# Scales of the input weights made for two blocks at once on GpSimd, with other paces beside the first attention

## The chip, the cores and the metric

One core of a Trainium2 chip runs the kernel. The core's engines each work through a queue of their own in order: TensorE (PE, matmuls; its weight loads are the row PEld), VectorE (DVE), ScalarE (ACT), GpSimd (POOL) and SyncE (SP, which here only issues DMAs; ACT issues some too). The metric is the device time of one execution in microseconds (us), the median of several runs.

## The reference, cut to what matters

Eight batches of sliding-window attention (8 heads, 576 positions, head size 64, window 128, a slope per head as bias), and on its output a bilinear feed-forward layer:

```python
scores = scale * np.matmul(q, k.transpose(0, 1, 3, 2))
mask = (rel >= 0) & (rel < window)
scores = np.where(mask, scores + bias[None], -1000000000.0)
attn = np.exp(scores - np.max(scores, axis=-1, keepdims=True))
attn = attn / (np.sum(attn, axis=-1, keepdims=True) + 1e-09)
...
x = attn_out.transpose(0, 2, 1, 3).reshape(B * S, H * D)   # attn_out = attn @ v
a = x @ w_a
b = x @ w_b
return (a * b @ w_out).astype(np.float32)
```

The float32 operands of most matmuls are split into two float16 parts, high and low, and a product is three matmuls (high by high, high by low, low by high). Each operand is first multiplied by a power of two that is made from its own norms.

## The kernel before

**Stages.** `first_attention` does batch 0's attention, four pairs of heads (p = 0 to 3) in four banks each, 16 turns in all. `first_batch` then runs the feed-forward layer of batch 0: `first_up` (12 blocks f of 128 hidden columns, 48 matmuls each, 576 in all, 49 steps), then `first_down` (24 steps of 12 matmuls). `batch(b)` does the same for batches 1 to 7. Beside the feed-forward layer of batch b runs the attention of later batches, `attention()`, in seventh parts of a pair of heads; `Pace.along(main, n, place)` steps it so that it stands at `place` pairs when the n steps of `main` are over. `weave(main, (side, a, z, steps))` spreads `steps` steps of `side` over the steps a to z of `main`.

**Weights.** The generator `weights` prepares the 12 blocks of the input weights (`up_weights`) and then the output weights (`down_weights`). It is stepped beside `first_attention` (`other(0.5)` is called 36 times and takes `rate` times a half step each time: 39 steps at a rate of 2.2), and then in `first_batch`. A block f goes through these stages:

- its two matrices are loaded (`load_weights`, L115, 512 KB each, from ACT's queue after the first three blocks) and put together from 64-bit words: ACT L126, DVE L127 and L129, two additions on POOL (L131);
- ACT squares them (L137), and PE adds the squares over the rows by four matmuls with ones (`up_norms`, L153, into a PSUM tile `wn_ps`);
- DVE takes the maximum of each matrix (L157, a reduction to `wtop`), and `power_scale` makes two scales of it in `sup`: L107 (clamp, factor), L109 (shift to the exponent), L110 (back to a float), all three on two columns;
- ACT writes the two high parts with the scale (L145), DVE the two low parts (L146, behind a pair of additions in `rest`).

**What sets the order.** Each engine's order is set when the kernel is compiled: a scheduler places instructions by its own simulated times. SP's order is written by hand in `first_attention` and `first_batch`, and PE's from batch 1 on; everything else is the scheduler's, so that a changed pace in one place can change the order of any engine nearby. `v`, the values of one batch for four pairs (1280 KB, L251), has one buffer: the next load waits until `split_x` has read what stands there. From batch 2 on, a pair's `qk` is split into `qkh` and `qkl` and laid out anew by four DMAs of SP's queue (L329 to L332), for which its score matmuls (L360) wait; `pT<-phl` (L383) is a transposing DMA of the probabilities.

## Time and profile before

| What | Value |
|---|---|
| median of 3 runs | 1061.12 us (1059.61 to 1067.57) |
| the profiled execution | 1065.21 us, its span 1063.4 us |
| PE busy | 991.9 us (93%) |
| DVE busy | 697.8 us (66%) |
| ACT busy | 649.3 us (61%) |
| POOL busy | 301.1 us (28%) |
| mean clock granted to PE | 0.973 of full speed |

The busy shares are means over the whole span. The stages differ: the views by window and by wait tell where PE, the busiest engine, stands still, and for whom. Times in the views are microseconds from the start of the span.

### The profile page before, as it was taken

The numbers are of one execution on the slowest core, as the hardware profiler recorded it, in microseconds if no ns is written. First come the engines' busy times: TensorE is split into PE (matmuls) and PEld (weight loads), VectorE is DVE, ScalarE is ACT, GpSimd is POOL, SyncE is SP. The second block draws the span as 40 slices with busy tenths as digits, with TensorE's granted clock in tenths as the row PEclk, the third lists the DMA queues.
The fourth block names the chain that finished last, engine by engine and source line by source line (L and its number), as shares of the span: only waits on it lengthen the run. The fifth ranks groups of instructions, "written<-read, shape, count | busy, mean of one in ns | idle before, by whom it ended". The sixth has DMA issues, their size and how long they took to land.

```text
span 1063.4 us, 23921 instructions
## 1 busy us (share of the span) xinstructions
PE 991.9 (93%) x9323; PEld 757.9 (71%) x9323; DVE 697.8 (66%) x1922; ACT 649.3 (61%) x1672; POOL 301.1 (28%) x331
## 2 busy tenths in 40 slices
PE   7678999979999899798999989999999989999998
PEld 5346667757776677575777767777777767777776
DVE  5999976446778646985777657775767576533530
ACT  6786777556767745666656666667656665523321
POOL 3444432100458304871112202230212212220110
PEclk8888999989999899998999999999999999999999
DMA  8344533653623633326423644335514733210000
GB/s 322 125 154 151 190 95 72 127 137 76 125 57 91 163 63 63 84 68 157 86 47 86 170 90 85 61 97 153 114 35 87 177 67 60 40 35 12 2 12 34
DMA packets 148433, 102.83 MB, mean 97 GB/s; under 512 B 120032, under 2 KB 128352, under 8 KB 147296
## 3 DMA queue, kind: packets, MB, share of 16 engines
q1 hardware_dynamic: 134496, 76.04, 31.6%
q10 hardware_dynamic: 13824, 25.27, 6.8%
q8 instruction: 73, 1.20, 0.5%
q14 instruction: 40, 0.33, 0.1%
HBM read 48.33 MB, written 9.44 MB: 54 GB/s over the span
## 4 chain that ended last, share of the span: by engine, by line
PE 46%; DVE 7%; ACT 7%; DMA 6%; issue 2%; SPq 0%; ACTq 0%; DVEq 0%
PE ch L776 15%; PE dn_ps L871 13%; PE p L776 11%; PE up_ps L776 3%; PE x_ps L473 2%; ACT phl L377 2%; DMA qk<-in_kT 2%; DMA v<-in_vP 2%; PE sc_ps L360 2%; DMA pT<-phl 1%; DVE phl L378 1%; DVE qkl L321 1%; ACT t L365 1%; ACT qkh L320 1%; DVE t L364 1%
## 5 line engine op out<-in xcount | busy, mean ns | idle before, releaser
L776 PEld LDWEIGHTS <-wup 128*128 128x128 f16 x4212 | 409.0, 99 | 145.5 <-issue 31.8
L871 PE MATMUL dn_ps<-h,wdn 128*128 128x288 f16 x2016 | 262.5, 289 | 2.3 <-DVE h L770 2.0
L776 PE MATMUL ch<-xs,wup 128*128 128x288 f16 x1584 | 231.1, 288 | 15.1 <-ACT rc L801 6.4
L871 PEld LDWEIGHTS <-wdn 128*128 128x128 f16 x2016 | 194.3, 99 | 58.1 <-issue 2.7
L776 PE MATMUL up_ps<-xs,wup 128*128 128x288 f16 x1440 | 189.1, 292 | 10.9 <-DVE v L590 4.1
L776 PE MATMUL p<-xs,wup 128*128 128x288 f16 x1188 | 178.9, 287 | 1.4 <-ACT rc L818 1.4
L365 ACT ACTIVATE t<-t,mn 128x192 f32<-128x192 f32 (+2 forms) x252 | 107.4, 427 | 73.6 <-DVE mn L364 72.8
L830 POOL TENSOR_TENSOR rc<-rc,row 128x288 f32<-128x288 f32 x66 | 60.1, 910 | 265.5 <-DVE row L828 233.7
L378 DVE SCALAR_TENSOR_TENSOR phl<-t,rin,phl 128x192 f16<-128x192 f32 (+2 forms) x252 | 105.9, 457 | 19.8 <-ACT phl L377 19.2
L377 ACT ACTIVATE phl<-t,rin 128x192 f16<-128x192 f32 (+2 forms) x252 | 88.9, 425 | 22.2 <-DMA pT<-phl 10.8
L769 ACT CAST h<-rc 128x576 f16<-128x576 f32 x96 | 64.0, 667 | 56.0 <-DVE rc L835 29.4
L770 DVE TENSOR_TENSOR h<-rc,h 128x576 f16<-128x576 f32 x90 | 73.0, 811 | 23.9 <-ACT h L769 22.7
L364 DVE CUSTOM_DVE_ANT_0 t<-sc_ps,bias,neg 128x192 f32<-128x192 f32 (+2 forms) x216 | 75.3, 389 | 19.6 <-PE sc_ps L360 19.5
L131 POOL TENSOR_TENSOR wup<-wup,wdn 128x512 int32<-128x512 int32 x36 | 51.9, 1464 | 66.1 <-ACT wdn L126 22.4
L408 DVE TENSOR_TENSOR xs<-v,xs 128x576 f16<-128x576 f32 x51 | 52.3, 1035 | 23.1 <-ACT xs L407 22.8
L807 DVE TENSOR_TENSOR rc<-p,rc 128x288 f32<-128x288 f32 x66 | 30.0, 455 | 52.6 <-PE p L776 50.8
L402 POOL TENSOR_TENSOR xq<-xq,sq 128x576 bf16<-128x576 bf16 x24 | 34.6, 1444 | 87.5 <-ACT sq L401 87.3
L875 ACT ACTIVATE row<-dn_ps,oi 128x288 f32<-128x288 f32 x56 | 27.6, 492 | 51.2 <-PE dn_ps L871 50.5
L812 ACT ACTIVATE row<-ch,g 128x288 f32<-128x288 f32 x66 | 32.6, 494 | 41.7 <-PE ch L776 41.2
L835 DVE SCALAR_TENSOR_TENSOR rc<-rc,g,ch 128x288 f32<-128x288 f32 x66 | 33.6, 509 | 35.1 <-PE ch L776 34.9
L360 PEld LDWEIGHTS <-qst 128*64 128x64 f16 x864 | 30.3, 110 | 32.4 <-issue 31.2
L234 POOL TENSOR_TENSOR wa<-wup 128x512 f32<-128x512 f16 x24 | 33.1, 1381 | 69.2 <-DVE phl L378 62.4
(137 smaller groups left out, 1337.2 us busy)
## 6 DMA issues: line engine op xcount, KB each, us to landing
v<-in_vP SPq DMA_DIRECT2D x8, 1280.0 KB, 6.6
out<-row ACTq DMA_DIRECT2D x64, 144.0 KB, 1.8
qk<-in_qT SPq DMA_DIRECT2D x28, 288.0 KB, 3.9
qk<-in_kT SPq DMA_DIRECT2D x28, 288.0 KB, 4.5
wdn<-in_w_out ACTq DMA_DIRECT2D x12, 512.0 KB, 5.3
wdn<-in_w_a ACTq DMA_DIRECT2D x9, 512.0 KB, 3.9
wdn<-in_w_b ACTq DMA_DIRECT2D x9, 512.0 KB, 4.8
qst<-qkh SPq DMA_DIRECT2D x24, 144.0 KB, 2.6
```

Of the source, the lines that this page charges most:

```text
L131: pool.tensor_tensor(out=t[:, m, :], in0=t[:, m, :], in1=low[:, m, :], op=ALU.add)
L360: pe.matmul(ps[64 * e:64 * e + 64, c:c + w], o.qs[:, e, qq], ks[:, e, kk], start=not last, stop=last)
L364: vec.tensor_tensor_reduce(out=t[:, c:c + w], in0=ps[:, c:c + w], in1=o.bias[:, WIN - w:WIN], scale=-0.125 if o.b == 1 else o.neg, scalar= ...
L365: act.activation(t[:, c:c + w], t[:, c:c + w], AF.Exp, bias=o.mn[:, n:n + 1], scale=-1.0, accum_out=o.sm[:, n:n + 1])
L377: act.activation(phl[:, 0, pc:pc + w], e, AF.Copy, scale=s)
L378: vec.scalar_tensor_tensor(out=phl[:, 1, pc:pc + w], in0=e, scalar=s, in1=phl[:, 0, pc:pc + w], op0=ALU.mult, op1=ALU.subtract)
L408: vec.tensor_tensor(out=xs[:, n, 1, :, :], in0=src, in1=xs[:, n, 0, :, :], op=ALU.subtract)
L769: act.copy(h[:, f, :, 0, :], hid)
L770: eng.tensor_tensor(out=h[:, f, :, 1, :], in0=hid, in1=h[:, f, :, 0, :], op=ALU.subtract)
L776: pe.matmul(ps[:, 0:HT], wup[:, a[0], a[1], wi, k, :], xs[:, b, xi, k, :], start=(first and n == 0), stop=(last and n == len(ks) - 1), ski ...
L830: pool.tensor_tensor(out=x0, in0=x0, in1=mid, op=ALU.mult)
L871: pe.matmul(ps[:, 0:HT], wdn[:, f, wi, e * P:(e + 1) * P], h[:, f, t, hi, :], start=(m == 0 and n == 0), stop=(m == NF - 1 and n == 2))
```

## The change

Scales are made for a group of two blocks: two blocks share one tile of PSUM, one reduction gives four columns, and `power_scale` runs on GpSimd (POOL), where the shift by 24 bits is a multiplication by 2^-24. The splitting of the two blocks, four pairs of instructions, follows over the next steps. `up_weights` has 56 steps in place of 52. The rate beside `first_attention` is 1.5 in place of 2.2 (27 steps in place of 39), the 50 steps beside `first_up` are spread over its steps 0 to 40 in place of 0 to 48, and the attention of batch 1 and 2 stands at 3.2 pairs in place of 2.8 after `first_up`, and at 5.15 in place of 4.9 after `first_down`. Line numbers behind the change are 4 or 5 higher: L126 is L130, L137 is L141, L145 is L149, L146 is L150, L157 is L161, L590 is L595.

```diff
--- before.py
+++ after.py
@@ -100,14 +100,18 @@
         vec.tensor_copy(c16, col)
         pe.matmul(dst, ones16, c16, start=True, stop=True)
 
-    def power_scale(dst, sq, slack, top):
+    def power_scale(dst, sq, slack, top, eng=vec):
 
         n = sq.shape[-1]
         cl = small.tile([P, n], F32, tag=f"cl{n}", name="cl")
-        vec.tensor_scalar(out=cl, in0=sq, scalar1=float(2.0**-40), scalar2=slack, op0=ALU.max, op1=ALU.mult)
+        eng.tensor_scalar(out=cl, in0=sq, scalar1=float(2.0**-40), scalar2=slack, op0=ALU.max, op1=ALU.mult)
         r = small.tile([P, n], I32, tag=f"r{n}", name="r")
-        vec.tensor_scalar(out=r, in0=cl.bitcast(I32), scalar1=24, scalar2=None, op0=ALU.logical_shift_right)
-        vec.tensor_scalar(out=dst.bitcast(I32), in0=r, scalar1=float(-(2**23)), scalar2=float((189 + top) * 2**23), op0=ALU.mult, op1=ALU.add)
+        if eng is pool:
+
+            eng.tensor_scalar(out=r, in0=cl.bitcast(I32), scalar1=float(2.0**-24), scalar2=None, op0=ALU.mult)
+        else:
+            eng.tensor_scalar(out=r, in0=cl.bitcast(I32), scalar1=24, scalar2=None, op0=ALU.logical_shift_right)
+        eng.tensor_scalar(out=dst.bitcast(I32), in0=r, scalar1=float(-(2**23)), scalar2=float((189 + top) * 2**23), op0=ALU.mult, op1=ALU.add)
 
 
     def load_weights(n, srcs, queue=act):
@@ -145,56 +149,57 @@
         act.activation(hi, x, AF.Copy, scale=s)
         return lambda: vec.scalar_tensor_tensor(out=lo, in0=x, scalar=s, in1=hi, op0=ALU.mult, op1=ALU.subtract)
 
-    def up_norms(f, sq):
-
-        ps = ps_at.tile([P, 512], F32, tag="at", name="wn_ps")
-        norms = ps[:, 0:2 * P].rearrange("p (m f) -> p m f", f=P)
+    def up_norms(f, sq, ps):
+
+        norms = ps[:, 2 * P * (f % 2):2 * P * (f % 2) + 2 * P].rearrange("p (m f) -> p m f", f=P)
         for c in range(NKC):
             pe.matmul(norms, ones16, sq[:, :, c * P:(c + 1) * P], start=(c == 0), stop=(c == NKC - 1))
 
-        def scale():
-            top = small.tile([P, 2], F32, tag="wtop", name="wtop")
-            vec.tensor_reduce(out=top, in_=norms, op=ALU.max, axis=AX)
-
-            power_scale(sup[:, f, :], top, 1.01, 14)
-
-        return scale
+    def up_scales(g, ps):
+
+        top = small.tile([P, 4], F32, tag="wtop", name="wtop")
+        vec.tensor_reduce(out=top, in_=ps.rearrange("p (m f) -> p m f", f=P), op=ALU.max, axis=AX)
+
+        power_scale(sup[:, 2 * g:2 * g + 2, :].rearrange("p f m -> p (f m)"), top, 1.01, 14, pool)
 
     def up_weights():
 
 
-        scale, sq, rest = {}, {}, []
-
-        def norms(f):
-            if f < NF:
-                scale[f] = up_norms(f, sq.pop(f))
-                if f + 3 < NF:
-                    load_weights(f + 3, (w_a[f + 3], w_b[f + 3]))
-                else:
-                    k = 2 * (f + 3 - NF)
-                    load_weights(f + 3, (w_out[k], w_out[k + 1]))
-
-        for f in range(NF + 1):
+
+        sq, rest, hi, ps = {}, [], [], None
+        for f in range(NF + 2):
             conv = convert(f) if f < NF else iter(())
             next(conv, None)
-            if f:
-                norms(f - 1)
+            n = f - 1
+            if 0 <= n < NF:
+                if n % 2 == 0:
+                    ps = ps_at.tile([P, 512], F32, tag="at", name="wn_ps")
+                up_norms(n, sq.pop(n), ps)
+                if n + 3 < NF:
+                    load_weights(n + 3, (w_a[n + 3], w_b[n + 3]))
+                else:
+                    k = 2 * (n + 3 - NF)
+                    load_weights(n + 3, (w_out[k], w_out[k + 1]))
             yield
             next(conv, None)
-            if f > 1:
+            if rest:
                 rest.pop(0)()
-            yield
-            if f:
-                scale.pop(f - 1)()
-                rest.append(split_up(f - 1, 0))
+            if 0 <= n < NF and n % 2:
+                up_scales(n // 2, ps)
+                hi += [(k, m) for k in (n - 1, n) for m in range(2)]
+            yield
+            if hi:
+                rest.append(split_up(*hi.pop(0)))
             yield
             if f < NF:
                 sq[f] = squares(f)
-            if f:
-                rest.append(split_up(f - 1, 1))
+            if hi:
+                rest.append(split_up(*hi.pop(0)))
+            if rest:
                 rest.pop(0)()
             yield
-        rest.pop(0)()
+        for _ in range(len(rest)):
+            rest.pop(0)()
 
     def down_weights():
 
@@ -917,7 +922,7 @@
     SP = {mybir.EngineType.SP}
     weights = chain(up_weights(), down_weights())
     with tc.manual_schedule(engines=SP):
-        first_attention(weights, 2.2)
+        first_attention(weights, 1.5)
     stack.close()
     hid = ctx.enter_context(tc.tile_pool(name="hid", bufs=1))
     h = hid.tile([P, NF, 2, 2, HT], F16, name="h")
@@ -936,8 +941,8 @@
         hidden_scale(st)
         for _ in split_x(st, True, False):
             pass
-        weave(att.along(first_up(st, h), 49, 2.8), (weights, 0, 48, 50))
-        weave(att.along(first_down(0, out_scale(st), h), 24, 4.9), (weights, 0, 12, 12))
+        weave(att.along(first_up(st, h), 49, 3.2), (weights, 0, 40, 50))
+        weave(att.along(first_down(0, out_scale(st), h), 24, 5.15), (weights, 0, 12, 12))
         for _ in weights:
             pass
 
```

**SP, the DMAs around the load of batch 2's values.** Before:

```order
L383 DMA_TRANSPOSE pT<-phl 128x32x128
L251 DMA v<-in_vP 128x2560
L329 DMA qst<-qkh 64x1152
L330 DMA qst<-qkl 64x1152
L331 DMA qkh<-qkh 64x1152
L332 DMA qkl<-qkl 64x1152
L293 DMA qk<-in_qT 64x2x576
L294 DMA qk<-in_kT 64x2x576
L383 DMA_TRANSPOSE pT<-phl 128x32x128
L293 DMA qk<-in_qT 64x2x576
L294 DMA qk<-in_kT 64x2x576
```

And now:

```order
L388 DMA_TRANSPOSE pT<-phl 128x32x128
L334 DMA qst<-qkh 64x1152
L335 DMA qst<-qkl 64x1152
L336 DMA qkh<-qkh 64x1152
L337 DMA qkl<-qkl 64x1152
L298 DMA qk<-in_qT 64x2x576
L299 DMA qk<-in_kT 64x2x576
L388 DMA_TRANSPOSE pT<-phl 128x32x128
L256 DMA v<-in_vP 128x2560
L298 DMA qk<-in_qT 64x2x576
L299 DMA qk<-in_kT 64x2x576
```

The load of `v` stands behind the four DMAs that lay out a pair, the two loads of `qk` and the transposing DMA; before, it stood ahead of all of them.

**ACT, the first pair of the first attention** (`vsq` is a sum of squares of `v`, of which four make its scale; `wdn<-in_w` are issued loads). Before:

```order
L260 ACTIVATE vsq,vs<-v 128x640
L137 ACTIVATE wdn<-wup 128x2x512
L260 ACTIVATE vsq,vs<-v 128x640
L585 COPY rin_397<-rin_ps 128x512
L585 COPY rin_397<-rin_ps 128x64
L115 DMA wdn<-in_w_a 128x512
L260 ACTIVATE vsq,vs<-v 128x640
L115 DMA wdn<-in_w_b 128x512
L126 ACTIVATE wdn<-wdn 128x1024
L145 ACTIVATE wup<-wup,sup 128x2x256 x2
L260 ACTIVATE vsq,vs<-v 128x640
L126 ACTIVATE wdn<-wdn 128x1024
```

And now:

```order
L265 ACTIVATE vsq,vs<-v 128x640
L141 ACTIVATE wdn<-wup 128x2x512
L265 ACTIVATE vsq,vs<-v 128x640
L590 COPY rin_363<-rin_ps 128x512
L590 COPY rin_363<-rin_ps 128x64
L265 ACTIVATE vsq,vs<-v 128x640
L130 ACTIVATE wdn<-wdn 128x1024
L265 ACTIVATE vsq,vs<-v 128x640
L130 ACTIVATE wdn<-wdn 128x1024
L141 ACTIVATE wdn<-wup 128x2x512
L119 DMA wdn<-in_w_a 128x512
L119 DMA wdn<-in_w_b 128x512
```

The two L145 and the two loads that stood ahead of the last `vsq` stand behind it, or later still.

**POOL and DVE, the last pair of the first attention** (L131, now L135, are the additions of a block; `cl`, `r` and `sup` the steps of a scale; L590, now L595, writes the attention's result into `v`). POOL before:

```order
L131 TENSOR_TENSOR wup<-wup,wdn 128x512 x2
L402 TENSOR_TENSOR xq<-xq,sq 128x576
L926 MEMSET phl 128x2x64
L926 MEMSET phl 128x2x128 x3
L926 MEMSET phl 128x2x64
L131 TENSOR_TENSOR wup<-wup,wdn 128x512 x2
```

POOL now:

```order
L407 TENSOR_TENSOR xq<-xq,sq 128x576
L135 TENSOR_TENSOR wup<-wup,wdn 128x512 x2
L107 TENSOR_SCALAR cl<-wtop 128x4
L931 MEMSET phl 128x2x64
L931 MEMSET phl 128x2x128 x3
L931 MEMSET phl 128x2x64
L111 TENSOR_SCALAR r<-cl 128x4
L135 TENSOR_TENSOR wup<-wup,wdn 128x512 x2
L114 TENSOR_SCALAR sup<-r 128x4
L407 TENSOR_TENSOR xq<-xq,sq 128x576 x2
```

DVE before, the end of the first attention:

```order
L129 SCALAR_TENSOR_TENSOR wup<-wdn,wup 128x2x512
L146 SCALAR_TENSOR_TENSOR wup<-wup,sup 128x2x256
L127 TENSOR_SCALAR wup<-wdn 128x2x512
L129 SCALAR_TENSOR_TENSOR wup<-wdn,wup 128x2x512
L157 TENSOR_REDUCE wtop<-wn_ps 128x2
L146 SCALAR_TENSOR_TENSOR wup<-wup,sup 128x2x256
L107 TENSOR_SCALAR cl<-wtop 128x2
L590 SCALAR_TENSOR_TENSOR v<-x_ps,sv,rin_845 128x512
L109 TENSOR_SCALAR r<-cl 128x2
L590 SCALAR_TENSOR_TENSOR v<-x_ps,sv,rin_845 128x64
```

DVE now:

```order
L131 TENSOR_SCALAR wup<-wdn 128x2x512
L580 RECIPROCAL rin_723<-rin_723 128x9
L133 SCALAR_TENSOR_TENSOR wup<-wdn,wup 128x2x512
L595 SCALAR_TENSOR_TENSOR v<-x_ps,sv,rin_659 128x512
L595 SCALAR_TENSOR_TENSOR v<-x_ps,sv,rin_659 128x64
L571 COPY pT<-tr_ps 128x512
L150 SCALAR_TENSOR_TENSOR wup<-wup,sup 128x2x256
L595 SCALAR_TENSOR_TENSOR v<-x_ps,sv,rin_746 128x512
L595 SCALAR_TENSOR_TENSOR v<-x_ps,sv,rin_746 128x64
```

The last step of the third group's scale (`sup<-r`) stands behind two additions of another block on POOL. On DVE, ahead of the last two L595, there stands one L150, which reads that scale.

## The prediction

> **What bounds the kernel now.** I began with the busy tenths of the page: over its 40 slices PE is full but for the first tenth of the span, and there DVE is the full one.
>
> ```profile
> PE   7678999979999899798999989999999989999998
> DVE  5999976446778646985777657775767576533530
> ```
>
> So I took the windows by stage: the end of the first pair of the first attention (25.5 us), the end of the first attention (89), and `first_up` to 181.3, in two parts and as a whole. The columns are busy us of PE, PEld, DVE, ACT and POOL, PE's granted clock and the DMA share.
>
> ```profile
> core 0: us, PE busy (x) PEld busy (x) DVE busy (x) ACT busy (x) POOL busy (x), PEclk, DMA share, GB/s
> 7.00:25.50 18.50, 12.08 (x124) 8.57 (x122) 13.37 (x38) 14.93 (x38) 5.95 (x5) 0.86 0.95 378
> 25.50:89.00 63.50, 42.40 (x387) 28.16 (x384) 60.35 (x138) 43.92 (x104) 31.66 (x27) 0.85 0.37 134
> 89.00:143.00 54.00, 50.03 (x409) 37.40 (x409) 46.20 (x115) 42.30 (x101) 20.04 (x14) 0.97 0.57 184
> 143.00:181.30 38.30, 38.30 (x361) 28.06 (x361) 27.65 (x80) 29.82 (x71) 10.17 (x9) 0.96 0.29 59
> 89.00:181.30 92.30, 88.33 (x769) 65.46 (x769) 73.85 (x193) 72.11 (x171) 30.21 (x23) 0.96 0.45 132
> ```
>
> From 25.5 to 89 us DVE works 60.35 of 63.50 us (95%), PE 42.40 and ACT 43.92: DVE is the bound there and PE is idle for 21 us. From 89 us PE is the bound: it idles 4.0 us up to 181.3. The two longest single waits of PE are in the view of waits (total, times, longest):
>
> ```profile
> PE vtot L267 <- DVE vc L264: 12.5, 4, 4.7
> ...
> PE sc_ps L360 <- DMA qkh<-qkh: 7.8, 2, 6.6
> ```
>
> The 4.7 us are the wait up to the first `vtot`, at 23.8 us, the 6.6 us for `qkh` lie at the start of batch 1, at 227.8 us. Behind that place the order of PE soon becomes the old one, so what is won or lost lies ahead of about 320 us, and the rest of the kernel moves with it.
>
> **Part 1: the first pair, -4.5 us.** PE's first scores of the second pair stand behind `vtot`, which waits for four sums of squares on ACT. ACT reached the last of them late:
>
> ```profile
> 18.10 0.74 ACT L260 ACTIVATE vsq<-v 128x640 bf16<-128x640 f32 x1 [1.62 <-DMA qk<-in_qT]
> ...
> 18.83 1.17 ACT L126 ACTIVATE wdn<-wdn 128x1024 int32<-128x1024 uint32 x1
> 19.86 1.35 ACT L145 ACTIVATE wup<-wup,sup 128x512 f16<-128x512 f32 x2
> 21.08 0.75 ACT L260 ACTIVATE vsq<-v 128x640 bf16<-128x640 f32 x1
> ...
> 23.54 0.16 DVE L264 CAST vc<-vs 128x4 bf16<-128x4 f32 x1
> ```
>
> In the new order the loads and the two L145 (1.62 us of waiting ahead of the third `vsq`, and 1.35) are behind the sums. ACT was free at 16.48 (18.10 less its wait): 0.74 + 1.17 + 0.75 more gives 19.1, in place of 23.54 when DVE, busy with L146, took them up. I take 4.5 us. At worst the second block's load is late and it is 3.
>
> **Part 2: the other three pairs, -11 us.** The DVE rows of the first 89 us that shrink:
>
> ```profile
> L129 DVE SCALAR_TENSOR_TENSOR wup<-wdn,wup 128x1024 int32<-128x1024 int32 x11 | 16.2, 1473 | 0.1
> L146 DVE SCALAR_TENSOR_TENSOR wup<-wup,sup 128x512 f16<-128x512 f32 x16 | 15.3, 958 | 3.0 <-ACT wup L145 3.0
> ...
> L127 DVE TENSOR_SCALAR wup<-wdn 128x1024 int32<-128x1024 int32 x11 | 8.4, 765 | 0.3 <-DMA wdn<-in_w_b 0.2
> L107 DVE TENSOR_SCALAR cl<-wtop 128x2 f32<-128x2 f32 x9 | 5.7, 630 | 0.1
> L109 DVE TENSOR_SCALAR r<-cl 128x2 int32<-128x2 int32 x9 | 4.1, 452 | 0.1
> L157 DVE TENSOR_REDUCE wtop<-wn_ps 128x2 f32<-128x256 f32 x9 | 3.7, 415 | 2.7 <-PE wn_ps L153 2.7
> L110 DVE TENSOR_SCALAR sup<-r 128x2 int32<-128x2 int32 x8 | 3.4, 429 | 0.1
> ```
>
> By the new order, three fewer each of L127 and L129 (0.765 + 1.473, 6.7 us) and seven fewer L146 (6.7) come before the end of this attention. All 26 instructions of the scales go to POOL (5.7 + 4.1 + 3.4 = 13.2). Nine reductions of 256 columns (3.7) become three of 512. A reduction of 512 columns and one of 64 take 0.81 together, so three cost at most 2.1, and that saves 1.6. In all DVE loses 28 us; about 4 of them lie ahead of 25.5 us, in part 1. DVE keeps 60.35 - 24 = 36 us. ACT loses two L126, two L137 and eight L145:
>
> ```profile
> L126 ACT ACTIVATE wdn<-wdn 128x1024 int32<-128x1024 uint32 x11 | 12.7, 1151 | 0.9 <-DMA wdn<-in_w_b 0.9
> ...
> L145 ACT ACTIVATE wup<-wup,sup 128x512 f16<-128x512 f32 x16 | 10.7, 718 | 1.7 <-DVE sup L110 1.7
> L137 ACT ACTIVATE wdn<-wup 128x1024 bf16<-128x1024 f32 x9 | 9.4, 1049 | 0.5 <-POOL wup L131 0.5
> ```
>
> This is 2.3 + 2.1 + 5.7 = 10, less the 1.35 of part 1: 35 us are left. PE keeps 42.40 less three blocks of norms (12 of the row below, 2.1 us): 40 us. So no engine is the bound by much; three share a chain (score, DVE, ACT, transpose, copy). If one engine could be 95% busy, as DVE was, the stretch would take 42 us. In the first stretch, where no engine led, the fullest was busy 14.93 of 18.5 (81%): 50 us. I add 2.5 us for a wait that the new order makes at the end. On DVE the last L595 stand behind an L150 that needs the third group's scale, and on POOL that scale stands behind two additions (2.5 us a pair in the last row below), then comes a scaling on ACT (0.7). I take 52.5 in place of 63.5. The ends are 42 (-21) and 61 (-2.5), three engines at 66%.
>
> ```profile
> L153 PE MATMUL wn_ps<-wdn,ones 128*128 128x256 bf16 x48 | 8.6, 311 | 3.0 <-ACT wdn L137 2.5 <-DVE mn L551 0.5
> 0.87 0.10 POOL L72 MEMSET halves<- 128x2 f32 x1
> ...
> 13.51 0.43 POOL L531 TENSOR_SCALAR bias<-rel_sb,sl_sb 128x192 f32<-128x192 f32 x1
> ...
> 28.71 2.52 POOL L131 TENSOR_TENSOR wup<-wup,wdn 128x512 int32<-128x512 int32 x2 [5.64 <-ACT t L552]
> ```
>
> The new work on POOL is 18 instructions of four columns. Between a memset of two columns (0.10) and a `tensor_scalar` of 192 (0.43) they cost 2 to 8 us in all, on an engine that is busy half of this stretch (31.66 of 63.50). I set it at nothing beside the 2.5 us above; its price is the waits in the third rival.
>
> **Part 3: `first_up`, +6 us.** What is deferred comes here: three blocks of norms on PE (+2.1, on the bound). DVE gets 13.4 us of L127, L129 and L146 more and 0.4 pairs of attention above 2.8 (about 3, if a third of the 73.85 was attention), less 2 for the scales: 73.85 + 15 = 89 of 94 us. ACT gets 10 and about 3: 85. Before, in 89 to 143, DVE was busy 46.2 of 54 (86%) and PE idle for 4.0, and from 143 to 181, at 72%, PE never waited. At 94% I expect about twice the idle time, 8 in place of 4. The ends are +2 (the norms alone) and +11 (DVE at 86%: 103.5 us for 92.3). The weights themselves come in time: in the new order the last norms stand behind 216 of the 576 matmuls of `first_up`, the output weights' total behind 474, which leaves 102 matmuls (13 us at 0.13, by the last row of part 4) ahead of `first_down`.
>
> **Part 4: the start of batch 1, -8 us.** SP's and PE's rows:
>
> ```profile
> 224.38 0.35 SPq L251 DMA_DIRECT2D v<-in_vP  x1
> ...
> 231.94 0.46 SPq L331 DMA_DIRECT2D qkh<-qkh  x1
> 234.54 6.53 SPq L383 DMA_TRANSPOSE pT<-phl  x1
> ...
> 252.30 0.51 SPq L329 DMA_DIRECT2D qst<-qkh  x1
> ...
> 255.51 0.51 SPq L332 DMA_DIRECT2D qkl<-qkl  x1
> ```
>
> ```profile
> 221.34 0.25 PE L360 MATMUL sc_ps<-qkl,qst 128*64 128x192 f16 x2
> ...
> 234.37 0.27 PE L360 MATMUL sc_ps<-qkh,qst 128*64 128x64 f16 x2 [6.55 <-DMA qkh<-qkh]
> ...
> 235.74 4.64 PE L776 MATMUL up_ps<-xs,wup 128*128 128x288 f16 x24
> ...
> 240.77 3.11 PE L776 MATMUL up_ps<-xs,wup 128*128 128x288 f16 x24
> ```
>
> At 224.38 the load of `v` got its buffer; the four layout DMAs were queued behind it (the third went out at 231.94 only), and PE stood for 6.55 us. In the new order they stand ahead of it. They then wait only for `qst`, which the matmuls of 221.34 release, and need some 6 us (252.30 to 255.51 for the four, and 2.4 to land, as from 231.94 to 234.37): 227.5. PE comes there 72 matmuls (0.13 each) after 221.6, at 231, and doesn't wait. With the wait goes the slower clock behind it (24 matmuls in 4.64, not 3.11). 6.55 + 1.5 is 8. The cost: `v` now goes out behind the transposing DMA (234.54 + 6.53, some 17 us later than before). In PE's order its first use, a `vtot`, stands 144 matmuls (19 us) and some scores behind those first scores, at 250 or later. `v` needs up to 7.6 us to arrive (224.38 to 231.94) and four sums of 0.75: 241 + 10.6 is about 252. This is close, but the transposing DMA was itself held up behind `v` and the layout before and can go out earlier. I take nothing. If `v` is late, the gain is gone. SP's queue behind `v` holds the next pair's loads, wanted a pair later.
>
> **The sum.** -4.5 - 11 + 6 - 8 = -17.5 us, so the profiled execution's 1065.2 would become 1047.7. That one lies 4.1 us over the median of the runs shown, so against the median 1061.1 I forecast 1043.6, rounded to 1044. The moved attention (0.25 pairs from batch 1 into batch 0's time) is the same PE work elsewhere: nothing, since both are bound by PE.
>
> **Rivals.**
> 1. Paid back in `first_up`: DVE or ACT becomes the bound there. For: 94% and 90% load in one stretch. Against: PE has five banks of slack there and stood only 4 us before. With parts 1 and 2 at -12, part 3 at +11 and part 4 at -8 it is -9: 1052.
> 2. The wait at the start of batch 1 only changes its name: `v` is late. For: SP's queue is in order, and `v` is behind a DMA that took 6.53 us of it. With part 4 at nothing it is -9.5: 1052.
> 3. Slower: the scales on POOL stand in ACT's way. ACT's four L149 of a group stand in its queue ahead of exponentials and of copies that free PE's banks, and all wait for POOL. The rows for the price:
>
> ```profile
> 28.95 1.07 DVE L107 TENSOR_SCALAR cl<-wtop 128x2 f32<-128x2 f32 x1
> ...
> 35.35 1.22 DVE L129 SCALAR_TENSOR_TENSOR wup<-wdn,wup 128x1024 int32<-128x1024 int32 x1
> ```
>
> A DVE instruction of two columns took 1.07 while POOL's two additions ran (from 28.71), and the cast of part 1, with four columns, 0.16: the two engines exclude each other. If each of a scale's three instructions waits out an L129 (1.22) and the group two additions (2.5), that is 6.2 us a group and 37 for six. This would give -17.5 + 37: 1081. It decides from 2.9 us shown on PE for each group. Against: only the third group has additions between its steps, and the splits stand one or more turns behind their reduction.
>
> The Trainium skill states this exclusion too (SBUF — State Buffer, section "Who interferes with whom"): the pair of ports that VectorE and GpSimd share is an exclusive lock, and a DVE instruction with two SBUF inputs contends with a GpSimd instruction that reads SBUF. The rows above agree. By that rule the lock that cost DVE 0.9 us at L107 now costs POOL, at the worst 18 times 1.22 or 22 us of its queue, and the time would be rival 3's only if all of that showed.
>
> **Chances and range.** The forecast (-11 us or more) 0.60; rival 1 0.17; rival 2 0.10; rival 3 0.08; losses or gains by the new order that I don't see 0.05, spread evenly. The likeliest time is 1044. With all ends of the parts at their best it is -4.5 - 21 + 2 - 8 = -31.5, with all at their worst -3 - 2.5 + 11 + 0 = +5.5. The low end of the range takes part 2 at -17 and part 3 at +3 (1034.6), the high end rivals 1 and 2 (1052) with part 2 worse by another 5: 1034 to 1057. About 1% (10.6 us) is what a measurement of this kernel can tell from no change: faster 0.62, same 0.28, slower 0.10.
>
> **What would show it.** Part 1: `vtot` near 19.3 us. Part 2: L595 of the last pair near 73 us, DVE no longer at 95%. Part 3: `first_up` lasts some 98 us, with DVE over 90%. Part 4: no wait of PE for `qkh` at the start of batch 1. The forecast is wrong if PE waits more than 15 us in `first_up`, or if ACT's L149 wait for `sup` in several groups.

## The result, and the profile after

| | before | after |
|---|---|---|
| time, median (range) of the runs | 1062.61 us (1059.61 to 1067.57, 7 runs) | 1054.47 us (1048.78 to 1058.66, 7 runs) |
| profiled execution, span | 1065.21, 1063.4 | 1050.78, 1049.0 |
| first `vtot` on PE | 23.75 | 19.46 |
| first attention's end (`up_ps` behind the last `v`) | 88.96 | 67.74 |
| first `dn_ps` (`first_down` begins) | 181.30 | 175.36 |
| first `up_ps` of batch 1 | 226.18 | 219.33 |
| first `dn_ps` of batch 1 (L871, now L876) | 317.30 | 305.22 |

The ratio is 0.9906 (95% interval 0.9877 to 0.9935). The kernel became 0.9% faster: 1054.5 lies in the range of the prediction, near its upper end, and 10 us over the forecast of 1044. By stages the two profiled executions differ by -4.3 (up to `vtot`), -16.9 (the rest of the first attention), +15.3 (`first_up`), -0.9 (`first_down`), -5.2 (batch 1 up to its `dn_ps`) and -2.3 behind that, in all -14.4. That is more than the -8.1 of the medians, since the profiled execution of before lies 2.6 over its median and that of after 3.7 under. Of all the runs below, one (1978.19 us, with the attention's place at 2.65) is in no median and no ratio.

The windows of after, cut at its own landmarks (columns as in the prediction):

```profile
core 0: us, PE busy (x) PEld busy (x) DVE busy (x) ACT busy (x) POOL busy (x), PEclk, DMA share, GB/s
20.20:67.74 47.54, 36.44 (x383) 24.99 (x380) 40.95 (x101) 40.95 (x101) 26.20 (x31) 0.89 0.39 142
67.74:175.36 107.62, 92.46 (x802) 67.63 (x801) 90.59 (x206) 80.16 (x188) 49.24 (x38) 0.95 0.56 143
```

From just behind `vtot` (20.20) to the end of the first attention DVE is busy 40.95 of 47.54 us (86%, it was 95%), and ACT exactly as long: the two are level now. `first_up` takes 107.62 us, and PE is idle for 15.2 of them (4.0 before), though DVE is busy only 84% and ACT 74%. Of the 15.3 us that this stage lost, 11.2 are idle time of PE. PE's largest waits, in the view of waits (total, times, longest):

```profile
PE up_ps L781 <- ACT rc L734: 7.9, 1, 7.9
...
PE rin_ps L586 <- DVE v L595: 4.3, 1, 4.3
...
PE x_ps L478 <- DVE vhl L283: 3.7, 1, 3.7
```

The 6.6 us for `qkh` at the start of batch 1 are gone from this list. New is the first row, one wait of 7.9 us in `first_up` (the 3.7 us lie there too, the 4.3 us ahead of it). Followed back in the timeline of after (start, duration, engine, line; in brackets how long the engine was idle and for whom; SPq and ACTq are DMAs, with the time for which each held the issuing engine's queue), PE waited for a copy on ACT, ACT for the buffer `phl`, and `phl` was being read by a transposing DMA:

```profile
102.19 19.81 SPq L388 DMA_TRANSPOSE pT<-phl  x1
...
99.64 0.82 ACTq L119 DMA_DIRECT2D wdn<-in_w_out  x2
100.55 0.87 ACTq L119 DMA_DIRECT2D wdn<-in_w_out  x2
...
104.61 0.33 ACTq L119 DMA_DIRECT2D wdn<-in_w_out  x1
104.98 0.73 ACTq L119 DMA_DIRECT2D wdn<-in_w_out  x1
...
124.15 0.64 ACT L382 ACTIVATE phl<-t,rin 128x64 f16<-128x64 f32 x2 [7.15 <-DMA pT<-phl]
...
125.73 0.37 ACT L734 COPY rc<-up_ps 128x288 f32<-128x288 f32 x1
...
126.16 4.96 PE L781 MATMUL up_ps<-xs,wup 128*128 128x288 f16 x24 [7.87 <-ACT rc L734]
```

The DMA that writes `pT` out of `phl` took 19.81 us of SP's queue; the 27 later ones of this run took 4.7 to 5.6. It went out at 102.19, in the middle of six loads of the output weights (512 KB each). Its counterpart in the kernel before took 4.94 us:

```profile
127.06 0.33 ACTq L115 DMA_DIRECT2D wdn<-in_w_out  x1
127.43 0.45 ACTq L115 DMA_DIRECT2D wdn<-in_w_out  x1
```

```profile
130.59 4.94 SPq L383 DMA_TRANSPOSE pT<-phl  x1
```

```profile
132.68 0.33 ACTq L115 DMA_DIRECT2D wdn<-in_w_out  x1
133.05 1.21 ACTq L115 DMA_DIRECT2D wdn<-in_w_out  x1
```

There is one `phl` in both kernels, so in after ACT's next L382 stood for 7.15 us, and behind it in ACT's queue the copy L734 that frees PE's bank. Before, two such loads went out 3 us ahead of the DMA and two 2 us behind; here it is four within 3 us ahead and two behind. So the theory for the tests: `first_up` lost what it lost over 6 us to this one meeting. The rival is the prediction's own reason, that DVE and ACT have too much to do in `first_up`.

### The profile page after: what moved, and what is told of

It is laid out like the page before. It is cut to its first block, busy times and chain, and to the rows that moved or that the text cites. A ratio compares the mean times of both kernels' runs of the same rounds, so it can differ in the third digit from the quotient of the medians.

```text
span 1049.0 us, 23864 instructions
## 1 busy us (share of the span) xinstructions
PE 982.9 (94%) x9323; PEld 752.5 (72%) x9323; DVE 688.6 (66%) x1880; ACT 647.5 (62%) x1672; POOL 311.9 (30%) x349
## 4 chain that ended last, share of the span: by engine, by line
PE 42%; ACT 5%; DVE 5%; DMA 4%; issue 2%; SPq 0%; ACTq 0%; DVEq 0%
PE ch L781 14%; PE dn_ps L876 13%; PE p L781 11%; PE x_ps L478 2%; DMA v<-in_vP 2%; DMA qk<-in_kT 2%; ACT phl L382 2%; PE sc_ps L365 2%; DVE phl L383 1%; DVE qkl L326 1%; ACT qkh L325 1%; DMA pT<-phl 1%; DVE t L369 0%; ACT vsq L265 0%; ACT t L370 0%
## 5 line engine op out<-in xcount | busy, mean ns | idle before, releaser
L876 PE MATMUL dn_ps<-h,wdn 128*128 128x288 f16 x2016 | 258.7, 287 | 1.2 <-DVE h L775 1.2
L876 PEld LDWEIGHTS <-wdn 128*128 128x128 f16 x2016 | 192.8, 98 | 55.2 <-issue 1.3
L382 ACT ACTIVATE phl<-t,rin 128x192 f16<-128x192 f32 (+2 forms) x252 | 88.7, 425 | 27.6 <-DMA pT<-phl 14.2
L135 POOL TENSOR_TENSOR wup<-wup,wdn 128x512 int32<-128x512 int32 x36 | 54.4, 1532 | 41.1 <-DVE wup L133 8.3
L407 POOL TENSOR_TENSOR xq<-xq,sq 128x576 bf16<-128x576 bf16 x24 | 37.1, 1544 | 91.4 <-ACT sq L406 91.1
L478 PE MATMUL x_ps<-pT,vhl 128*64 128x128 f16 (+3 forms) x1176 | 46.6, 229 | 3.7 <-DVE vhl L283 3.7
```

The lines of the kernel that those rows point to most:

```text
L135: pool.tensor_tensor(out=t[:, m, :], in0=t[:, m, :], in1=low[:, m, :], op=ALU.add)
L382: act.activation(phl[:, 0, pc:pc + w], e, AF.Copy, scale=s)
L478: pe.matmul(xp[oc // 512][64 * h:64 * h + 64, o0:o0 + w], vt[0:rows, c:c + 64], probs(pt, rows, blocks, h), start=(n == 0 and first), stop ...
L876: pe.matmul(ps[:, 0:HT], wdn[:, f, wi, e * P:(e + 1) * P], h[:, f, t, hi, :], start=(m == 0 and n == 0), stop=(m == NF - 1 and n == 2))
```

## The experiments

All ratios are to the kernel before, timed on the same chip as the run. The runs came in three groups, each on a chip of its own, so two kernels are compared by their ratios.

**The size of the loads.** Three runs are about the meeting. In the first the loads of the output weights are cut to an eighth of their columns:

```
-            queue.dma_start(raws[n % 3][:, m, :], src)
+            w = DM if n < NF else DM // 8
+            queue.dma_start(raws[n % 3][:, m, 0:w], src[:, 0:w])
```

> This is the changed kernel, but each load of the output weights brings only the first eighth of its columns, 64 KB in place of 512 KB; the rest of what is computed there is left undefined, and the output is not the reference's. The order of the instructions is that of the changed kernel. Theory A: the 15 us that first_up got longer (the prediction had 6) come from one transposing DMA that meets six output-weight loads, takes 19.8 us of SP's queue in place of 5, and holds ACT (7.15 us) and, behind it, PE (7.87 us). Then here that DMA takes 5 to 6 us, ACT's wait for pT is under 1 us, first_up lasts 97 to 100 us in place of 107.6, and the time is 7 to 11 us under the changed kernel's, some 1045 (0.983 of the kernel before). Theory B (the prediction's reason: DVE and ACT have too much to do in first_up): first_up stays at 105 us or more and the time within 3 us of 1054. Theory C: the DMA is slow by something else than the loads (its own data, or where it starts): it still takes over 12 us.

Measured: 1043.35 us, 0.9797 (0.9773 to 0.9821). SP's timeline of this run:

```profile
103.55 5.50 SPq L389 DMA_TRANSPOSE pT<-phl  x1
```

The DMA stands at the same place in the order and takes 5.50 us. ACT's wait and PE's 7.87 are gone, `first_up` lasts from 68.93 to 169.18, 100.3 us in place of 107.6. Theory A held: `first_up` is just over its 100, and the time 11 us under the changed kernel's. But this kernel leaves out seven eighths of the output weights, so it can't say that nothing else was won.

**The place of the loads.** Everything is loaded, but the first six loads go out on SP's queue, in order with the transposing DMA:

```
-                    load_weights(n + 3, (w_out[k], w_out[k + 1]))
+                    load_weights(n + 3, (w_out[k], w_out[k + 1]), sp)
```

> The changed kernel, with the first six loads of the output weights (three blocks) issued on SP's queue in place of ACT's; everything is loaded and computed. In SP's order two of them now stand ahead of the first transposing DMA of the second attention and four behind it, so that they no longer share the DMA engines with it. Theory A (the transposing DMA among the loads is what first_up lost): that DMA takes 5 to 7 us of SP's queue in place of 19.8, ACT's wait of 7.15 us and PE's of 7.87 us are gone, first_up lasts 98 to 102 us, and the time is 5 to 10 us under the changed kernel's: about 1046, 0.981 to 0.986 of the kernel before. Rival B: the loads now come so late that ACT stands for them at the conversion of an output block (L130), and what is won at the transposing DMA is lost there: within 3 us of the changed kernel. Rival C: SP's queue stands for a free buffer of the weights, and the transposing DMA goes out later than 110 us: PE waits for pT, time 1055 or more.

Measured: 1044.03 us (1042.06 to 1045.29), 0.9782 (0.9766 to 0.9799). SP's timeline, and the window of `first_up`:

```profile
99.66 0.80 SPq L119 DMA_DIRECT2D wdn<-in_w_out  x2
105.02 5.63 SPq L388 DMA_TRANSPOSE pT<-phl  x1
110.76 1.93 SPq L119 DMA_DIRECT2D wdn<-in_w_out  x4
```

```profile
70.58:170.28 99.70, 90.27 (x802) 66.63 (x801) 90.54 (x204) 79.31 (x186) 49.93 (x37) 0.98 0.51 154
```

Two loads, the transposing DMA in 5.63 us, then four loads: they follow one another. `first_up` takes 99.7 us, and PE idles 9.4 of them. Theory A held in the trace; of rival B there is 2.07 us of ACT waiting for a load, without a loss that the time shows. The gain is larger than A's 5 to 10 us: 1.2%, some 13. Between the two profiled executions `first_up` accounts for 7.9 us of it; where the rest lies is not shown. This is the fastest of the kernels that compute everything, by one word. Its five runs also scatter less (3 us) than the seven of the changed kernel (10).

Is the move to SP's queue worth something by itself? The same edit on the kernel before:

> The kernel before, with the six loads on SP's queue and nothing else. Its first transposing DMA of the second attention took 4.94 us already. Theory A: nothing is won: 0.998 to 1.002. Rival B: the loads on SP's queue are worth something by themselves: 0.996 or less. Rival C: SP's queue stands for free buffers of the weights, and it is slower: 1.004 or more.

Measured: 1066.34 us, 1.0011 (0.9995 to 1.0027). Theory A: nothing.

**The time of the transposing DMA.** One number changed in the changed kernel, so that the attention runs slower beside `first_up`:

```
-        weave(att.along(first_up(st, h), 49, 3.2), (weights, 0, 40, 50))
+        weave(att.along(first_up(st, h), 49, 2.65), (weights, 0, 40, 50))
```

> The changed kernel with one number changed: the second attention's place at the end of first_up is 2.65 in place of 3.2. In ACT's and SP's order the first transposing DMA of the second attention then comes later against the loads of the output weights; by the changed kernel's pace (34.4 us behind the start of first_up at 3.2) near 41 us, when the six loads should have landed. Theory A: that DMA takes 5 to 7 us, and the time is 4 to 9 us under the changed kernel's (0.982 to 0.987 of the kernel before). Rival B: the attention that is put off costs the same again at the start of batch 1, where qkh is late once more: within 3 us of the changed kernel. Rival C: the DMA still meets loads and takes over 10 us.

Measured: 1062.0 us, 0.9954 (0.9931 to 0.9978). My estimate of the place was wrong. SP's timeline, then ACT's:

```profile
105.69 18.58 SPq L388 DMA_TRANSPOSE pT<-phl  x1
```

```profile
124.11 1.14 ACT L130 ACTIVATE wdn<-wdn 128x1024 int32<-128x1024 uint32 x1 [4.42 <-DMA wdn<-in_w_out]
...
134.05 1.10 ACT L130 ACTIVATE wdn<-wdn 128x1024 int32<-128x1024 uint32 x1 [7.04 <-DMA wdn<-in_w_out]
```

The DMA went out 37 us behind the start of `first_up` (68.60), not 41, met the loads again and took 18.58 us. Rival C, then: the gain that A expected did not come, and the meeting stayed. Here the loads are the ones that ACT stands for, 4.42 and 7.04 us: both sides of the meeting are slow. The attention that was put off costs something too, as in rival B: `first_down` takes 51.7 us in place of 44.0, with 504 matmuls in place of 450, while `first_up`, with fewer of them, is still 2.5 us longer than the changed kernel's. In all this kernel is 0.5% slower than the changed one.

**The parts of the change.** The new paces alone, with `up_norms`, `power_scale` and `up_weights` as before:

```
-        first_attention(weights, 2.2)
+        first_attention(weights, 1.5)
...
-        weave(att.along(first_up(st, h), 49, 2.8), (weights, 0, 48, 50))
-        weave(att.along(first_down(0, out_scale(st), h), 24, 4.9), (weights, 0, 12, 12))
+        weave(att.along(first_up(st, h), 49, 3.2), (weights, 0, 40, 50))
+        weave(att.along(first_down(0, out_scale(st), h), 24, 5.15), (weights, 0, 12, 12))
```

> The kernel before, with the new paces alone: 1.5 weight steps beside a step of the first attention, and the new numbers for first_up and first_down; each block still gets its own scale at once, on VectorE. Theory A: the paces carry most of the change: vtot comes at 19 to 20 us, the first attention ends at 70 to 75 us (88.96 before, 67.74 changed), and the time is 1054 to 1058, 0.992 to 0.996 of the kernel before. Rival B: without the grouping on GpSimd the paces bring little: the first attention ends after 80 us, or what it wins is lost again in first_up, and the time is 1060 or more.

Measured: 1052.32 us, 0.9882 (0.9859 to 0.9905): a little faster than A expected, and not slower than the whole change. `vtot` comes at 19.80, the first attention ends at 74.84, and the transposing DMA takes 5.67 us: without the grouping, the loads stand elsewhere. The other part, the grouped scales on GpSimd with the old paces (the changed kernel with the minus lines of this diff):

> The changed kernel's grouped scales on GpSimd with the old numbers of the paces (2.2 weight steps; 2.8 and 48 steps; 4.9). The kernel with the new paces alone came to 0.988 of the kernel before. Theory A: the paces carry the gain, and this comes within 4 us of the kernel before (0.996 to 1.004): DVE is relieved by the scales of some 8 us in the first attention, but stays near 90%, and vtot stays at 23 to 24 us. Rival B: the grouping alone brings half or more of the gain: 0.994 or less. Rival C: it is slower than the kernel before by over 4 us, as ACT's L149 of a pair of blocks stand ahead of exponentials.

Measured: 1065.25 us, 0.9981 (0.9966 to 0.9997). Theory A in the time: with the old paces the grouping on GpSimd brings 0.2% (`vtot` comes at 21.75, earlier than A has it).

Then the changed kernel with the grouped scales on VectorE:

```
-        power_scale(sup[:, 2 * g:2 * g + 2, :].rearrange("p f m -> p (f m)"), top, 1.01, 14, pool)
+        power_scale(sup[:, 2 * g:2 * g + 2, :].rearrange("p f m -> p (f m)"), top, 1.01, 14)
```

> The changed kernel, with the grouped scales computed on VectorE in place of GpSimd: same order of blocks, same paces. It tells what GpSimd itself brings. Theory A: the gain of the first attention comes from the weight steps that are put off, and GpSimd's part is small: 18 small instructions come back to DVE, 9 of them in the first attention, at about 0.45 us each, some 4 us; the first attention ends at 69 to 72 us in place of 67.7 and the time is 0 to 4 us over the changed kernel's (about 1056). Rival B: taking the scales off DVE is the main thing: the first attention ends at 76 us or later and the time is 1060 or more. Rival C: GpSimd's scales cost more than they bring, as the last additions stand ahead of the third group's scale there: the wait of 4.3 us of PE at the end of the first attention goes and the time is 2 to 4 us under the changed kernel's.

Measured: 1057.62 us (1048.49 to 1061.68), 0.9927 (0.9898 to 0.9956). The first attention ends at 71.07, as A has it, but the time can't be told from the changed kernel's, and here too the transposing DMA met loads (12.08 us). The grouped scales take DVE only 2.4 us there, in nine steps. So GpSimd was measured once more with the meeting away, by the same edit on the kernel with the loads on SP's queue:

> The kernel of the run before this one, with the grouped scales on VectorE in place of GpSimd. With the collision away from both, the difference of the two is what GpSimd itself brings. Theory A: little: the first attention ends 2 to 5 us later (DVE has 8 us more to do there by the windows of the two kernels with the collision: 50.67 and 58.76 us busy), and the time is 2 to 5 us longer. Rival B: nothing: first_up takes it back, within 1.5 us. Rival C: over 6 us longer.

Measured: 1050.39 us, 0.9852 (0.9834 to 0.9869), against 0.9782 with GpSimd: 0.7% or 6.4 us between the medians. That is just over A, at the low edge of C. The window of its `first_up`:

```profile
71.55:177.43 105.88, 93.14 (x802) 68.20 (x802) 90.55 (x214) 80.88 (x193) 42.08 (x28) 0.96 0.47 145
```

The first attention ends only 1 us later than with GpSimd (71.55, 70.58), so it is not there that the time is lost: `first_up` takes 105.88 us in place of 99.70. PE idles 12.7 us there and not 9.4, and works 93.1 and not 90.3, at a granted clock of 0.96 in place of 0.98. DVE is busy the same 90.5 us in both. The largest wait that is new stands in PE's timeline, and what caused it in ACT's:

```profile
100.20 0.60 PE L156 MATMUL wn_ps<-wdn,ones 128*128 128x256 bf16 x4 [3.92 <-ACT wdn L141]
```

```profile
98.05 1.16 ACT L130 ACTIVATE wdn<-wdn 128x1024 int32<-128x1024 uint32 x1 [2.42 <-DMA wdn<-in_w_b]
```

PE waits 3.92 us for the squares of a block (L141). They stand in ACT's queue behind L130 of the last block, and that waited 2.42 us for its load. The load went out 18.2 us behind the start of `first_up` (at 89.78) and landed 8.2 us later; with the scales on GpSimd it went out 16.2 us behind it (86.77), and ACT did not wait. So the 3.3 us that PE idles more in this stage come, once more, from a load that the order placed later. What the relief of DVE is worth by itself these runs don't show.

And the new paces alone, with the loads on SP's queue as well:

> The new paces alone, each block's scale at once on VectorE (0.988 of the kernel before), with the six loads on SP's queue as well. In the kernel of the paces alone the transposing DMA took 5.67 us already, so it lost nothing to the loads. Theory A: nothing is won: within 2 us of 0.988, and the change's grouping on GpSimd, with the loads on SP, is worth the whole of what lies between 0.978 and this. Rival B: the loads on SP's queue win something by themselves (ACT is rid of six issues, or they come earlier): 0.984 or less.

Measured: 1051.07 us, 0.9868 (0.9847 to 0.9889). Theory A. With the loads on SP's queue the parts now stand in a row:

| with the six loads on SP's queue | ratio |
|---|---|
| the kernel before | 1.0011 |
| and the new paces | 0.9868 |
| and the scales by two blocks, on VectorE | 0.9852 |
| and these on GpSimd | 0.9782 |

The paces bring 1.4%, the move to GpSimd, with the order that comes with it, 0.7%, the grouping nothing that can be told. With the loads where the change left them, the same row is 1, 0.9882, 0.9927, 0.9906: the grouping moves the loads to where the transposing DMA is, and that took back about what GpSimd brought.

**Two waits that stay.** The load of `v` ahead of the transposing DMA at the start of batch 1:

```
             if p == 1 and b > 1:
-                st = load_v(b)
+                st = ahead
...
                 hidden_scale(st)
+                if b < B:
+                    ahead = load_v(b)
```

> The changed kernel, with one swap on SP's queue at the start of batch 1: the load of v is issued ahead of the transposing DMA at 214 us, not behind it; the whole output is computed. Theory A: the 2.98 us wait of PE at 229 us and the slower clock behind it (about 1.5 us) come from v, which ACT waits for at 226 us. Then that wait is gone and the next landmarks lie 3 to 5 us earlier against the end of first_up, time about 1050 (0.987 of the kernel before). Rival B: v must wait for its buffer, and holds the transposing DMA and all behind it in SP's queue: PE waits for pT or qkh instead, time 1054 to 1060. Rival C: PE's wait at 229 has another cause, nothing changes within 1.5 us.

Measured: 1053.4 us, 0.9885 (0.9858 to 0.9913), not to be told from the changed kernel. SP's, ACT's and PE's timelines in this order:

```profile
218.14 0.54 SPq L256 DMA_DIRECT2D v<-in_vP  x1
218.78 9.74 SPq L388 DMA_TRANSPOSE pT<-phl  x1
```

```profile
226.98 0.74 ACT L265 ACTIVATE vsq<-v 128x640 bf16<-128x640 f32 x1 [3.73 <-DMA v<-in_vP]
```

```profile
228.58 3.10 PE L783 MATMUL up_ps<-xs,wup 128*128 128x288 f16 x24 [3.00 <-ACT row L769]
```

The time doesn't decide between A and C, since A's 0.987 lies in the interval as well. The trace does: the wait stays, as in C, but its cause is no other, it is still `v`'s. The load went out 6 us earlier against the start of batch 1 (218.14 with 223.93; 219.55 with 219.33 in after). But the transposing DMA now runs beside it (9.74 us, not 5.50), `v` takes 8.8 us to arrive in place of 6.8, and in the new order ACT comes to it earlier. What did go is the slow stretch behind the wait: 24 matmuls take 3.10 us there, not 4.64, and batch 1 up to its `dn_ps` takes 84.4 us in place of 85.9. The total hides it, since `first_up` is 3.4 us longer in this run.

Last, the scale of the third group alone on VectorE, on the kernel with the loads on SP's queue:

```
-        power_scale(..., top, 1.01, 14, pool)
+        power_scale(..., top, 1.01, 14, vec if g == 2 else pool)
```

> The kernel with the six loads on SP's queue (0.978 of the kernel before), with the scale of the third group alone computed on VectorE; the five others stay on GpSimd. It tests the 4.3 us for which PE waits at the end of the first attention: the last writes of v (L595) stand on DVE behind an L150 that needs this scale, and on GpSimd the scale's last step stands behind two additions of 2.5 us. Theory A: the three steps take 1.5 us on DVE, there is no addition ahead of them, PE's wait falls to 2 us or less and the first attention ends 2 to 3 us earlier; the time is 1 to 3 us less. Rival B: DVE itself is late there: PE's wait stays over 3.5 us and the time is the same within 1.5 us. Rival C: the end of the first attention comes earlier but first_up takes it back, since DVE and ACT then have the same work in a shorter stretch.

Measured: 1047.91 us, 0.9831 (0.981 to 0.9852), slower than without the edit (0.9782). That is neither A's time nor B's; the two profiled executions lie 2.0 us apart. PE's and DVE's timelines:

```profile
63.33 2.19 PE L586 MATMUL rin_ps<-ident,rin 64*64 64x64 f32 x36 [4.45 <-DVE v L595]
...
72.78 4.08 PE L781 MATMUL up_ps<-xs,wup 128*128 128x288 f16 x32 [3.40 <-DVE v L595]
```

```profile
62.47 0.16 DVE L114 TENSOR_SCALAR sup<-r 128x4 int32<-128x4 int32 x1
...
63.99 4.13 DVE L150 SCALAR_TENSOR_TENSOR wup<-wup,sup 128x512 f16<-128x512 f32 x3
68.21 0.70 DVE L131 TENSOR_SCALAR wup<-wdn 128x1024 int32<-128x1024 int32 x1
68.94 1.22 DVE L133 SCALAR_TENSOR_TENSOR wup<-wdn,wup 128x1024 int32<-128x1024 int32 x1
70.20 1.87 DVE L150 SCALAR_TENSOR_TENSOR wup<-wup,sup 128x512 f16<-128x512 f32 x1
71.99 0.93 DVE L595 SCALAR_TENSOR_TENSOR v<-x_ps,sv,rin 128x512 f32<-128x512 f32 x2
```

The scale is ready at 62.6 (its last step on GpSimd ended at 65.8 in the kernel without the edit), but PE's wait stays (4.45), as in rival B, and a second of 3.40 comes: DVE now has four L150 and the steps of another block (L131, L133) ahead of the last L595. The first attention ends at 72.78, 2.2 us later than without the edit.

The expectation had the wrong wait. PE's and DVE's timelines of after show which L595 stands behind what:

```profile
61.47 2.01 PE L586 MATMUL rin_ps<-ident,rin 64*64 64x64 f32 x36 [4.34 <-DVE v L595]
...
67.74 4.18 PE L781 MATMUL up_ps<-xs,wup 128*128 128x288 f16 x32 [0.59 <-DVE v L595]
```

```profile
59.54 1.22 DVE L133 SCALAR_TENSOR_TENSOR wup<-wdn,wup 128x1024 int32<-128x1024 int32 x1
60.67 0.94 DVE L595 SCALAR_TENSOR_TENSOR v<-x_ps,sv,rin 128x512 f32<-128x512 f32 x2
...
65.61 0.75 DVE L150 SCALAR_TENSOR_TENSOR wup<-wup,sup 128x512 f16<-128x512 f32 x1 [3.40 <-ACT wup L149]
66.93 0.94 DVE L595 SCALAR_TENSOR_TENSOR v<-x_ps,sv,rin 128x512 f32<-128x512 f32 x2 [0.57 <-PE x_ps L478]
```

PE's 4.34 us are for the L595 at 60.67, which stands behind L133 and other work on the blocks, not behind the scale. The L150 that needs the scale was late by 3.40 us, but not for the scale either: that was ready at 63.58, and ACT took the squares of a block first (L141, itself behind a copy of 0.70 us that waited for PE up to 63.31):

```profile
63.90 1.07 ACT L141 ACTIVATE wdn<-wup 128x1024 bf16<-128x1024 f32 x1
64.86 2.55 ACT L149 ACTIVATE wup<-wup,sup 128x512 f16<-128x512 f32 x4
```

And the L595 at 66.93 had to wait for PE's own `x_ps` another 0.57 us. So the place of the scale behind the two additions delayed nothing, and moving it could win nothing.

## Why the prediction was right, and where it was wrong

**Part 1** (-4.5): right, -4.3. PE's wait for the first `vtot` fell from 4.73 to 0.61 us.

**Part 2** (-11): right in kind, too small. It was -16.9. I took an engine at 81% and 52.5 us for the stretch behind `vtot`. In after that stretch takes 47.5, with DVE and ACT at 86%. The loads of the engines were not as counted: DVE and ACT are busy 41 us each (36 and 35 in the prediction), and PE 36 (40). The 2.5 us for the third group's scale were a term that measured nothing. GpSimd's timeline has the additions ahead of the scale's last step:

```profile
60.90 2.52 POOL L135 TENSOR_TENSOR wup<-wup,wdn 128x512 int32<-128x512 int32 x2
63.38 0.20 POOL L114 TENSOR_SCALAR sup<-r 128x4 int32<-128x4 int32 x1
```

But the scale was there 1.3 us before ACT came to its L149, and the last L595 waited for PE's `x_ps` in any case (the rows at the end of the experiments).

What carried the part was placed less well. Of the 28 us that DVE was to lose it lost 23 (busy 73.8 us up to the end of the first attention before, 50.7 in after), and the prediction gave 13.2 of them to the scales on GpSimd. With the new paces alone DVE is busy 60.2 us up to there, with the grouping as well 58.8, and only 2.4 of these are scales; the rest of the 8.1 that the move to GpSimd brings is mostly steps of blocks that come later in its order. The paces alone bring the end from 88.96 to 74.84 (-14.1), the grouping and GpSimd the other 7.1 in this run. In the runs with the scales of after it lies between 67.7 and 70.6, at a granted clock of 0.90 to 0.83 up to there. At 0.83, near the 0.84 of the paces alone, it lies between 68.9 and 70.6, and 4 to 6 us of the 7.1 are left.

**Part 3** (+6): this step failed, in size and in reason. It was +15.3. "DVE over 90%" is not what the windows show (84%); PE's idle 15.2 us are over the prediction's own mark of 15 for being wrong. The part priced norms and the load of DVE and ACT, and put what the denser steps do to the DMAs at nothing: six loads come within 5.5 us and a transposing DMA among them, and PE stands for 7.87 us at one place. The trace before could not show the price, since its loads stood farther apart and the DMA took 4.94. With the meeting away, the loss is the predicted one: +7.9 with small loads (100.3 less 92.3), +7.4 with the loads on SP's queue (99.7), where DVE is at 91% and PE's largest wait in `first_up` (3.24 us) is for a row of DVE. So what is left is of the size that part 3 forecast, with DVE's share near its 94%; beside it lay a loss as large that it did not have.

**Part 4** (-8): half right. The wait for `qkh` is gone, and the stage is 5.2 us shorter. A new wait took part of it. ACT's and PE's timelines:

```profile
226.38 0.74 ACT L265 ACTIVATE vsq<-v 128x640 bf16<-128x640 f32 x1 [2.87 <-DMA v<-in_vP]
```

```profile
229.21 4.64 PE L781 MATMUL up_ps<-xs,wup 128*128 128x288 f16 x24 [2.98 <-ACT row L767]
```

This is rival 2 in another place, at a smaller price: `v` is late not for `vtot` but for a `vsq` in ACT's queue (2.87 us), ahead of the rows L767 that free PE's banks; PE waits 2.98 and then runs 24 matmuls in 4.64 us. The prediction followed `v` to its first use on PE and not to its first use on ACT. The slow matmuls are not bound to the wait: with `v` issued earlier PE waited 3.00 us and then ran 24 in 3.10.

**The rivals.** Rival 1 gave 1052, and the time is nearer to it than to the forecast. But its mechanism, DVE or ACT as the bound, is not what gave the gain back, as the kernel with the loads on SP's queue shows: the same instructions on DVE and ACT, and 2.2% under the kernel before, where the forecast had 1.6%. Without the meeting the sum would have been somewhat too small, by part 2. That the time lies in the range as it is owes something to luck: part 2 gave 5.9 us more than forecast, not by its own count, and this covers most of the 9.3 that part 3 cost beyond its 6. Rival 3 did not happen: L149 waits for `sup` once, for 1.33 us, and 18 steps on GpSimd take 7.3 us in all, within the 2 to 8 of the prediction:

```profile
L111 POOL TENSOR_SCALAR r<-cl 128x4 int32<-128x4 int32 x6 | 3.4, 570 | 0.4
...
L107 POOL TENSOR_SCALAR cl<-wtop 128x4 f32<-128x4 f32 x6 | 2.4, 404 | 13.1 <-DVE wtop L161 13.1
...
L114 POOL TENSOR_SCALAR sup<-r 128x4 int32<-128x4 int32 x6 | 1.5, 252 | 0.4
```

By the prediction's estimate the Trainium skill's rule (SBUF — State Buffer, section "Who interferes with whom"), that the ports which the two engines share are an exclusive lock, would have cost GpSimd at most 22 us here. The mean of 0.57 us for L111 against 0.25 for L114, of the same size, may be such waits (not shown), but nothing near the bound. On DVE the trace agrees with the rule: two L150, which read two tiles of SBUF each, took 3.14 us (from 55.57) while GpSimd's additions ran (55.19 to 58.17), and one took 0.75 when GpSimd was idle (65.61). The L107 that the prediction showed reads one tile and says nothing on the part about two.

## What to carry to other kernels

When a change moves compute work closer together, list the DMAs that the moved steps issue and see which others go out in the same 20 us: the price may lie there and not on the engines. Here a transposing DMA whose source has a single buffer ran beside bulk loads, and putting both on one queue, in the order in which they are needed, won 1.2%. When a change gains less than its parts, measure each part with the suspected loss taken away. And follow a wait to the end of its chain before a cure is tried: the 4.3 us that were put down to a late scale hung on other work.

## What the runs showed of the hardware

The time of a transposing DMA (`phl` to `pT`, 1 MB) on SP's queue depends on what else is under way. It is 4.7 to 6.5 us everywhere else in the kernels before and after, 9.74 beside the load of `v` (1.3 MB), and 12.08, 17.75, 18.58 and 19.81 among loads of the output weights from ACT's queue. It is more than sharing. The rates in GB/s from 95 to 130 us, in 40 slices of 0.875 us, in after and then in the kernel with the loads on SP's queue:

```profile
GB/s 0 0 0 0 0 0 84 379 398 365 229 267 318 359 153 5 18 49 55 48 201 59 128 120 71 194 160 228 194 138 157 289 204 316 335 267 379 398 103 33
```

```profile
GB/s 0 0 0 0 0 0 94 351 403 337 14 0 26 140 4 164 290 290 290 112 304 426 398 356 417 370 28 179 387 197 272 361 379 112 5 0 0 0 0 75
```

In the second, two loads take four slices at some 350, the DMA shows as the stretch at 290, and the four other loads follow at 300 to 426: 3.5 us, and 12.7 us from the DMA's issue at 105.02 to the last bytes, 16 in all. In after the same work begins at 100.25, sinks to 5 to 55 GB/s from 108 to 112 us, and the DMA lands at 124.1: 24 us. That the slow stretch is not an empty one shows the DMA share, 0.76 from 108 to 112 us at 32 GB/s.

The Trainium skill says (DMA: Bandwidth & Descriptors, section "Queues, rings and completion order") that a DMA engine takes turns between the queues it has work for, packet by packet. By that rule alone the two would stretch each other and, as an estimate from the rates above, be done together after some 16 us; the trace has 24. What the rest is lost to was not tried.
